# Fetching residual tiles one by one under two down products, and moving two tiles' LayerNorm statistics from VectorE to ScalarE

## The chip, the cores and the metric

One core of one Trainium2 chip. The metric is the device time of one execution in microseconds (us); lower is better. The kernel before takes 1430.34 us (median of 3 runs, 1430.0 to 1430.77). A verdict "faster" or "slower" needs 2%, 28 us; this study is about 2 us, so its conclusions rest on traces more than on times. In the lines of the profile PE is TensorE, PEld its weight loads, DVE VectorE, ACT ScalarE, POOL GpSimd and SPq the issuer of the DMA queue (SyncE); L428 is line 428 of the kernel, and brackets hold the idle time before an instruction and what ended it.

## The reference, cut to what matters

```python
x = A_x                                                  # 2048 x 1024, bf16
x = x + _A_ref(_layernorm(x, axis=-1), A_wqkv, A_wo)     # linear attention
x = x + _B_ref(_layernorm(x, axis=-1), B_w_gate, B_w_up, B_w_down)
x = x + _A_ref(_layernorm(x, axis=-1), A_wqkv, A_wo)
x = x + _B_ref(_layernorm(x, axis=-1), B_w_gate, B_w_up, B_w_down)
# _B_ref: g = x @ w_gate; u = x @ w_up; (g * u) @ w_down, inner width 3584
```

## The kernel before: the parts that matter

The tokens are 16 tiles of 128 rows. The multiplications of layer B are done with seven block products in place of eight, so PE has fewer columns to carry, at the price of additions and subtractions on VectorE. A layer B has two passes (`ps_` 0 and 1) over 8 tiles each: gate and up products, then a *down stage* of seven products in the order "1", "2", "6", "7", "4", "5", "3", four row tiles t each. That makes four down stages in a run. The residual tiles of a pass (`x_res`, 256 KB each) are overwritten as scratch space in the gate-up part of three of the four passes; they are stashed in DRAM and fetched back in the down stage.

All transfers that the kernel issues go through one queue (319.34 of the 320.74 MB in the profile; the rest is on two queues that it calls "instruction"), and SyncE issues them in the order in which the program has them (the burst below from 1107.59 us, the transposes behind it from 1112.33). The helper `P.add` records an instruction with what it reads and writes, and the waits follow from that.

```python
def tail(part):                     # end of the gate-up work, put under the first down product
    ...
    if part < 3:
        return
    for _ in range(2 if "R1" not in order else 1):
        ring_issue()                # weight fetches, 5 slots in a ring
    for t in range(8 if l2 and not jit else 0):
        i = 8 * ps_ + t
        dma(x_res[:, i, :], xscr[i * 128:(i + 1) * 128, :], r_x(i), KX[i], rd=R(V_X + i * 32, 32))

def evac(t, q=q):                   # after each row tile t of a product q
    ...
    if q == "1":
        P.add("act", ...copy bank to bank...)
        tt(hd, hd, hc, ALU.add, ...)             # two VectorE passes of 1.08 us
        tt(ha, hd, ha, ALU.subtract, ...)
    elif q in "24":
        stt(xs, pb, CD, a, ra_, rx, prd=[bank])  # residual tile += product
    elif q in "67":
        stt(rtmp[k], pb, CD, xs, rx, rr(k), prd=[bank])
        if q == "6":
            tt(hb, hb, ha, ALU.subtract, ...)
            tt(ha, hc, ha, ALU.subtract, ...)    # the operand of product "7"
    ...
    ticks(q, t)                     # in the first pass: lnp.flush_step() under "1" and "2"
    l2_ops(q, t)                    # operands of later products
```

`flush_step` finishes the LayerNorm of the last tiles in three steps: statistics (`start`; VectorE's BN_STATS, or two ScalarE passes with an accumulator, `ln_s1` and `ln_s2`: 1.06 and 1.15 us, each with 0.19 us for a separate instruction that reads the accumulator), normalize (`b2_one`, on VectorE, into one of a few buffers), and a transpose by the DMA engines (`step_t`) which reads that buffer. Tile 14 is normalized into the buffer that the transpose of tile 12 reads.

Of the kernel before, what the change touches and what calls it, by code (L numbers as in the profile page):

```python
# [180 lines left out]
def build_kernel(nc, A_x, A_wqkv, A_wo, B_w_gate, B_w_up, B_w_down, out):  # L181
# [97 lines left out]
    V_X = TOTAL + 64  # L279
# [46 lines left out]
    with ExitStack() as es:  # L326
# [82 lines left out]
        def R(o, n):  # L409
            return [(o, o + n)]  # L410

        def r_x(i, lo=0, hi=D):
            return [(O_X + (i * D + lo) * 2, O_X + (i * D + hi) * 2)]
# [13 lines left out]
        def dma(dst_ap, src_ap, wr, key, rd=()):  # L427
            P.add("sp", lambda e: e.dma_start(dst_ap, src_ap), rd=rd, wr=wr, dma_sem=key)  # L428
# [71 lines left out]
        class LN:  # L500
# [21 lines left out]

            def start(self, i, mid=None):
                assert i == self.n
                if self.to == "A0" and i in LN_ACT or self.to == "A" and i < 12:
                    j = ln_s1(self.order[i], *self.junk(i))
                    self.q_s.append((i, j))
                else:
                    j = ln_a(self.order[i], mid)
                self.n += 1  # L530
                self.q_b.append((i, j))
# [98 lines left out]

            def flush_step(self):
                self.step_t(1)
                if self.q_n:
                    self.b2_one()
                    self.b1_one()
                else:
                    self.b1_one()
                    self.b2_one()
                if self.n < NST and self.pending_ab() < 3:
                    self.start(self.n)  # L640

# [741 lines left out]
        def layer_B(lnp, nxt, first):  # L1383
# [207 lines left out]
            def gateup(ps_, ticks, l2):  # L1591
                jit = first and ps_ == 0
                NP = NU // 2
                pairs = [pair(ps_, p, l2) for p in range(NP)]

                def step(p, q, i):
                    L = pairs[p]["L"]
                    if q in L:
                        L[q]["st%d" % i]()

                order = ORDERS[not first, ps_].split()

                def sums(p, q):
                    if p < NP:
                        pairs[p]["sums"](q, "make" if first else "load")

                n0 = ps_ * NPASS

                pre = ("P1A", "P1B", "P5A", "P5B")
                tpl = tp_ops(ps_, l2)  # L1610
                todo = [(q, k) for q in dict.fromkeys(tk[0] for tk in order if tk[0] in l2) for k in range(4)]
                plain = set()

                def tp_next(q0=None):
                    for q, k in list(todo):
                        if (q == q0) if q0 else (k < 3 or q in plain):
                            assert k < 3 or q in plain
                            todo.remove((q, k))
                            tpl[q][k]()
                            if not q0:  # L1620
                                return

                def emit(p, tk, head=False):
                    late_ = tk[-1] == "'"
                    if late_:
                        p, tk = p - 1, tk[:-1]
                    if p < 0:
                        return
                    if p == 0 and not head and tk in pre:
                        if late_ and tk[:2] == "P5":  # L1630
                            pairs[0]["c22"]("AB".find(tk[-1]))
                        return
                    if p == 1 and tk[0] in l2 and tk[1] == "1":
                        tp_next(tk[0])
                    c, x = pairs[p], "AB".find(tk[-1])
                    if tk[0] == "P":
                        c["p" + tk[1]](x)
                    elif tk[0] == "D":
                        c["fin"](tk[1], x)()
                    elif tk[0] in "1245":  # L1640
                        step(p, tk[0], int(tk[1]))
                    elif tk[0] == "R":
                        if p or tk == "R1":
                            ring_issue()
                    elif tk == "W":
                        wd_dma()
                    elif tk[0] == "S" and not (early and p == 0):
                        sums(p + (tk[2] == "+"), tk[1])
                    elif tk[0] == "T":
                        i = int(tk[1])  # L1650
                        if jit:
                            store_s(n0 + 2 * p + i)
                            if p + 1 < NP:
                                prep_s(n0 + 2 * p + 2 + i)
                        ticks(2 * p + i)
                    if p == 0 and tk in ("P1B", "P5B", "D2B", "D4B") and tk[1] in l2:
                        plain.add(tk[1])
                    if p == 0 and not head:
                        tp_next()

                early = not first
                if early:
                    for q in "25"[ps_:]:
                        sums(1, q)
                for tk in pre:
                    emit(0, tk, True)
                if ps_ == 0:
                    lnp.b2_one()
                    lnp.start(13)
                for p in range(NP):  # L1670
                    for tk in order:
                        emit(p, tk)

                late = [tk for tk in order if tk[-1] == "'"]
                late = [tk for tk in late if tk[:2] == "D2"] + [tk for tk in late if tk[:2] != "D2"]
                nd2 = sum(tk[:2] == "D2" for tk in late)

                def tail(part):
                    n = -(-(len(late) - nd2) // 3)
                    lo, hi = (0, nd2) if part == 0 else (nd2 + n * (part - 1), min(nd2 + n * part, len(late)))  # L1680
                    for tk in late[lo:hi]:
                        emit(NP, tk)
                    if part < 3:
                        return
                    for _ in range(2 if "R1" not in order else 1):
                        ring_issue()
                    for t in range(8 if l2 and not jit else 0):
                        i = 8 * ps_ + t
                        dma(x_res[:, i, :], xscr[i * 128:(i + 1) * 128, :], r_x(i), KX[i], rd=R(V_X + i * 32, 32))
                return tail  # L1690

            def down(ps_, ticks, tail):
# [150 lines left out]
                for qi, q in enumerate(DPROD):  # L1843
# [17 lines left out]
                    def evac(t, q=q):  # L1861
                        pb, bank = psb((B_DX if q in "1674" else B_DV)[t]), (B_DX if q in "1674" else B_DV)[t]
                        ha, hb, hc, hd = [v[:, :, t * 128:(t + 1) * 128] for v in (hA, hB, hC, hD)]
                        ra, rb, rc, rd_ = [rh(x, t) for x in (O_HA, O_HB, O_HC, O_HD)]
                        if q == "1":
                            P.add("act", (lambda d, b: lambda e: e.copy(psb(d), psb(b)))(B_DV[t], bank), prd=[bank], pwr=[B_DV[t]])
                            tt(hd, hd, hc, ALU.add, rd_ + rc, rd_)
                            tt(ha, hd, ha, ALU.subtract, ra + rd_, ra)
                        elif q in "24":
                            sh = "24".index(q)  # L1870
                            xs, rx = xq(sh, 0, t)
                            a, ra_ = r4[t] if q in l2d else (xs, rx)
                            stt(xs, pb, CD, a, ra_, rx, prd=[bank])
                            final(sh, 0, t)
                        elif q in "67":
                            sh = "67".index(q)
                            xs, rx = xq(sh, 1, t)
                            k = t if sh else 4 + t
                            stt(rtmp[k], pb, CD, xs, rx, rr(k), prd=[bank])
                            if q == "6":  # L1880
                                tt(hb, hb, ha, ALU.subtract, ra + rb, rb)
                                tt(ha, hc, ha, ALU.subtract, ra + rc, ra)
                        else:
                            sh = "35".index(q)
                            xs, rx = xq(sh, 1, t)
                            k = t if sh else 4 + t
                            stt(xs, pb, CD, rtmp[k], rr(k), rx, prd=[bank])
                            final(sh, 1, t)
                        ticks(q, t)
                        l2_ops(q, t)  # L1890

                    if q in l2d:
# [178 lines left out]
```

## Time and profile before

| | kernel before |
|---|---|
| time | 1430.34 us |
| span of the profiled run | 1429.3 us |
| PE busy | 1421.5 us, 99% |
| PE idle between its first and last matmul | 3.8 us |
| of it in the last layer's first down stage | 1.66 + 0.50 us |
| a residual tile, issue to landing, median | 6.1 us |

The lines that carry this, and how they are read, are in the prediction.

### The profile page before, as it was taken

The page shows a single profiled execution, that of the slowest core. Times are in us where ns is not written, and L with a number is a line of the kernel's source. Part 1 is how long each engine was busy: PE and PEld are TensorE (multiplying, and loading weights), DVE is VectorE, ACT ScalarE, POOL GpSimd, SP SyncE. Part 2 cuts the span into 40 slices and gives each one's busy share as a digit, 9 for nine tenths or more (in the row PEclk, how much of TensorE's full clock was granted, in tenths as well). Part 3 has the DMA queues.
Part 4 walks back from the last instruction along what each step waited for, and adds up shares of the span by engine and source line. Part 5 has one row for each costly group of instructions (what it writes and reads, how often), then busy time and mean ns, then how long its engine had stood idle before and what let it go on. Part 6 is the DMA issues. An engine that isn't in the chain of part 4 may idle for free.

```text
span 1429.3 us, 21974 instructions
## 1 busy us (share of the span) xinstructions
PE 1421.5 (99%) x8209; PEld 790.0 (55%) x8209; DVE 1205.5 (84%) x2356; ACT 712.5 (50%) x1455; POOL 154.5 (11%) x193
## 2 busy tenths in 40 slices
PE   9999999999999999999999999999999999999999
PEld 4444444555546566664554444456666475666548
DVE  7897978999888799987689978888888787888888
ACT  5882355444410266655377714567775004777400
POOL 3203521000010000002010045300000100000000
PEclk9999999999999999999999999999999999999999
DMA  7868979997786776769784366767775976777653
GB/s 237 222 142 221 217 177 203 300 316 265 251 263 211 239 255 243 257 222 303 230 280 104 101 173 167 167 197 259 245 255 197 273 255 231 257 263 254 208 194 122
DMA packets 270699, 320.74 MB, mean 224 GB/s; under 512 B 164096, under 2 KB 211072, under 8 KB 270592
## 3 DMA queue, kind: packets, MB, share of 16 engines
q1 hardware_dynamic: 270592, 319.34, 73.1%
q8 instruction: 64, 1.05, 0.3%
q14 instruction: 43, 0.35, 0.1%
HBM read 236.45 MB, written 73.40 MB: 217 GB/s over the span
## 4 chain that ended last, share of the span: by engine, by line
PE 86%; DVE 7%; issue 2%; ACT 2%; POOL 1%; DMA 1%; SPq 0%; POOLq 0%; DVEq 0%
PE ps L1419 28%; PE ps L1502 17%; PE ps L1854 13%; PE ps L1235 8%; PE ps L974 8%; PE ps L1761 6%; PE ps L1337 4%; DVE arena L806 3%; DVE arena L455 2%; PE ps L947 1%; DMA arena<-arena 1%; DVE arena L809 1%; POOL arena L466 1%; PE ps L1261 1%; PE ps L1288 0%
## 5 line engine op out<-in xcount | busy, mean ns | idle before, releaser
L806 DVE TENSOR_TENSOR arena<-arena 128x512 f16<-128x512 f16 (+7 forms) x1027 | 507.2, 522 | 57.2 <-ACT arena L1506 32.7
L1419 PE MATMUL ps<-arena 128*128 128x512 f16 x1888 | 457.1, 379 | 0.5 <-DVE arena L809 0.4
L809 DVE SCALAR_TENSOR_TENSOR arena<-ps,arena 128x512 f16<-128x512 f32 (+3 forms) x558 | 358.4, 658 | 76.8 <-PE ps L1854 36.8
L1502 PE MATMUL ps<-arena 128*128 128x256 f16 x2184 | 287.5, 273 | 0.0
L1419 PEld LDWEIGHTS ps<-arena 128*128 128x128 f16 (+1 forms) x1888 | 182.6, 98 | 163.2 <-ACT ps L1448 3.8
L1502 PEld LDWEIGHTS ps<-arena 128*128 128x128 f16 (+1 forms) x2184 | 211.9, 98 | 90.6 <-ACT arena L1506 6.9
L1854 PE MATMUL ps<-arena 128*128 128x512 bf16 (+1 forms) x1064 | 232.6, 379 | 1.7 <-DVE arena L806 1.7
L1854 PEld LDWEIGHTS ps<-arena 128*128 128x128 f16 x1064 | 103.8, 98 | 125.9 <-DVE arena L806 2.2
L1424 ACT ACTIVATE arena<-ps 128x512 f32<-128x512 f32 x224 | 133.7, 597 | 76.8 <-PE ps L1419 62.9
L1506 ACT ACTIVATE arena<-ps 128x256 f32<-128x256 f32 x351 | 125.1, 384 | 26.4 <-PE ps L1502 21.5
L974 PE MATMUL ps<-arena 128*128 128x512 f16 (+1 forms) x616 | 134.7, 380 | 0.6 <-ACT arena L981 0.6
L1235 PE MATMUL ps<-arena 128*128 128x512 bf16 x512 | 116.1, 379 | 0.0
L1337 PE MATMUL ps<-arena 128*128 128x512 bf16 x512 | 110.8, 379 | 0.0
L1512 ACT COPY ps<-ps 128x256 f32<-128x256 f32 x182 | 66.4, 365 | 75.3 <-DVE arena L809 28.6
L974 PEld LDWEIGHTS ps<-arena 128*128 128x128 f16 x616 | 59.3, 98 | 74.9 <-ACT arena L981 5.8
L1761 PE MATMUL ps<-arena 128*128 128x256 f16 (+1 forms) x882 | 97.2, 273 | 0.5 <-DVE arena L809 0.5
L1448 ACT COPY ps<-ps 128x512 f32<-128x512 f32 x112 | 65.4, 584 | 62.2 <-PE ps L1419 51.9
L1076 POOL TENSOR_TENSOR arena<-arena 128x1024 f16<-128x1024 f32 x32 | 76.2, 2381 | 156.7 <-DVE arena L1074 141.2
L1761 PEld LDWEIGHTS ps<-arena 128*128 128x128 f16 x882 | 86.0, 98 | 11.9 <-DVE arena L809 1.0
L1515 DVE TENSOR_TENSOR ps<-ps,arena 128x256 f32<-128x256 f32 x182 | 76.7, 428 | 10.6 <-PE ps L1502 9.6
L1337 PEld LDWEIGHTS ps<-arena 128*128 128x128 f16 x512 | 50.0, 98 | 60.5
L1789 ACT COPY arena<-ps 128x256 f32<-128x256 f32 x8 | 3.0, 372 | 158.3 <-PE ps L1761 158.3
(72 smaller groups left out, 980.5 us busy)
## 6 DMA issues: line engine op xcount, KB each, us to landing
arena<-w_scratch SPq DMA_DIRECT2D x84, 896.0 KB, 4.5
arena<-t_scratch SPq DMA_DIRECT2D x32, 896.0 KB, 6.0
arena<-in_B_w_down_dram SPq DMA_DIRECT2D x24, 896.0 KB, 5.2
arena<-sp_scratch SPq DMA_DIRECT2D x26, 768.0 KB, 4.2
w_scratch<-arena SPq DMA_DIRECT2D x28, 512.0 KB, 6.2
arena<-w_scratch SPq DMA_DIRECT2D x28, 384.0 KB, 5.1
x_scratch<-arena SPq DMA_DIRECT2D x40, 256.0 KB, 5.0
arena<-x_scratch SPq DMA_DIRECT2D x40, 256.0 KB, 6.1
```

Of the source, the lines that this page charges most:

```text
L806: P.add("dve", lambda e: e.tensor_tensor(out=out, in0=a, in1=b, op=op), rd=rd, wr=wr, prd=prd)
L809: P.add("dve", lambda e: e.scalar_tensor_tensor(out=out, in0=a, scalar=sc, in1=b, op0=ALU.mult, op1=op1), rd=rd, wr=wr, prd=prd)
L974: P.add("pe", lambda e: [e.matmul(psb(bank), a[0][:, k, :], b[0][:, k, :], start=(q in (1, 5) and k == 0), stop=(k == 3), skip_group_check ...
L1235: return [e.matmul(psb(bank), xrt[t][:, jj * 128:(jj + 1) * 128], pk[:, h, t, :], start=(t == tok[0]), stop=(t == tok[NST - 1])) for t in ts]
L1337: return [e.matmul(psb(bank), xnT[:, g, i * 128:(i + 1) * 128], wp[:, g, dh * 512:(dh + 1) * 512], start=(dh == 0 and g == 0), stop=(g == ...
L1419: P.add("pe", lambda e: [e.matmul(psb(bank), w[:, k, :], x[:, k, :], start=(start and k == 0), stop=(k == 3), skip_group_check=True) for k ...
L1424: P.add("act", lambda e: e.activation(t, psb(bank), AF.Copy, scale=SG), prd=[bank], wr=r)
L1502: P.add("pe", lambda e: [e.matmul(psb(bank)[:, 256 * half:256 * half + 256], w[:, k, :], xx[:, k, :], start=(start and k == 0), stop=(k == ...
L1506: P.add("act", lambda e: e.activation(d, src, AF.Copy, scale=sc), prd=[xk], wr=rd_)
L1515: P.add("dve", lambda e: e.tensor_tensor(out=half(c, 1), in0=U, in1=c5, op=ALU.add), prd=[xk], rd=rc5, pwr=[dst[c]])
L1761: P.add("pe", lambda e: [e.matmul(psb(bank)[:, 256 * half:256 * half + 256], a[:, k, 128 * r:128 * r + 128], b[:, k, :], start=(start and ...
L1854: P.add("pe", lambda e: [e.matmul(psb(bank), hv[:, 7 * hf + k, t * 128:(t + 1) * 128], w[:, k, :], start=(q in "15" and hf == 0 and k == 0 ...
```

## The change

Intent: the burst of eight fetches stands in the queue ahead of the LayerNorm transposes and of later weights, so it is spread, one fetch for each row tile of products "1" and "2"; and the last two tiles' statistics leave VectorE (busy for 14.21 of the 22 us from 1105, and waiting for 6.31 more) for ScalarE (busy for 2.28 of them).

```diff
@@ LN.start
-                if self.to == "A0" and i in LN_ACT or self.to == "A" and i < 12:
+                if self.to == "A0" and i in LN_ACT or self.to == "A" and i < 12 or self.to == "B" and i >= 14:
                     j = ln_s1(self.order[i], *self.junk(i))
@@ LN.flush_step
                 self.step_t(1)
-                if self.q_n:
+                n = len(self.q_n)
+                if n:
                     self.b2_one()
+                if self.q_b and (not self.q_s or self.q_s[0][0] > self.q_b[0][0]):
                     self.b1_one()
-                else:
-                    self.b1_one()
+                if not n:
                     self.b2_one()
+                self.s2()
@@ tail
-                    for t in range(8 if l2 and not jit else 0):
-                        i = 8 * ps_ + t
-                        dma(x_res[:, i, :], xscr[i * 128:(i + 1) * 128, :], r_x(i), KX[i], rd=R(V_X + i * 32, 32))
@@ evac
                         ticks(q, t)
+                        if q in "12" and (ps_ or not first):
+                            i = i0 + 4 * "12".index(q) + t
+                            dma(x_res[:, i, :], xscr[i * 128:(i + 1) * 128, :], r_x(i), KX[i], rd=R(V_X + i * 32, 32))
                         l2_ops(q, t)
```

## The prediction

> **What bounds the kernel now.** I read the page's engine table first, then the waits of PE, then the waits of the one stretch that holds PE's longest idle time, and there the timeline engine by engine. From the page (engine, busy us, share of the span):
>
> ```profile
> span 1429.3 us, 21974 instructions
> PE 1421.5 (99%) x8209; PEld 790.0 (55%) x8209; DVE 1205.5 (84%) x2356; ACT 712.5 (50%) x1455; POOL 154.5 (11%) x193
> ```
>
> PE is idle for 1429.3 - 1421.5 = 7.8 us in all. A busy PE need not be a fast one, so I checked its pace: the timeline has 56 matmuls of 512 columns that take 12.26 us (the PE line at 1140.57 below). The last one's record is 0.38 us long, so the 55 steps before it take (12.26 - 0.38) / 55 = 216 ns each. Going through the start times of all 512-column matmuls gives a median of 216 ns and hardly any outlier. So PE runs at its pace everywhere, and the change removes no matmul. Of the 7.8 us, 1.4 us lie before the first matmul and 2.7 us after the last (it ends at 1426.6). What is left, 3.8 us, is all that any change of waits can win. The waits of PE over the whole run (waiter, what it waited for, us in total, times, longest):
>
> ```profile
> PE ps L1854 <- DVE arena L806: 1.7, 1, 1.7
> PE ps L435 <- POOL arena L431: 1.4, 1, 1.4
> PE ps L974 <- ACT arena L981: 0.6, 3, 0.2
> PE ps L1761 <- DVE arena L809: 0.5, 1, 0.5
> PE ps L1419 <- DVE arena L809: 0.4, 1, 0.4
> ```
>
> L1854 is a plain down product and L1761 a down product split once more: two of the waits, 1.7 and 0.5 us, belong to the code that the change touches. Both fall in the first down stage of the last layer, at 1138.9 and 1156.7 us. The waits of that stretch (1105 to 1160) name where they start:
>
> ```profile
> DVE arena L496 <- DMA arena<-arena: 6.3, 1, 6.3
> PEld ps L1854 <- DMA arena<-t_scratch: 0.2, 1, 0.2
> ```
>
> The timeline shows the sequence (start, duration, engine, line; SPq is the DMA queue's issuer):
>
> ```profile
> 1107.21 0.34 SPq L428 DMA_DIRECT2D arena<-t_scratch  x1
> 1107.59 4.39 SPq L428 DMA_DIRECT2D arena<-x_scratch  x8
> 1112.33 10.51 SPq L579 DMA_TRANSPOSE arena<-arena  x3
> 1121.04 0.55 DVE L496 TENSOR_SCALAR arena<-arena 128x1024 f16<-128x1024 bf16 x1 [6.31 <-DMA arena<-arena]
> 1122.89 1.06 SPq L428 DMA_DIRECT2D arena<-t_scratch  x2
> 1128.30 0.68 DVE L809 SCALAR_TENSOR_TENSOR arena<-ps,arena 128x512 bf16<-128x512 f32 x1
> 1138.30 2.21 DVE L806 TENSOR_TENSOR arena<-arena 128x1792 f16<-128x1792 f16 x2
> 1140.57 12.26 PE L1854 MATMUL ps<-arena 128*128 128x512 f16 x56 [1.66 <-DVE arena L806]
> ```
>
> Eight residual tiles (256 KB each, 2 MB) are issued in one go. The transpose of a LayerNorm tile that was ready goes out 4.7 us later, behind them; the normalize of tile 14 (L496) needs the buffer which that transpose reads, so DVE stands for 6.31 us. [...] all its later work slides: the evacuation of product "2" starts at 1128.30, and the two subtractions that make the operand of product "7" end at 1138.30 + 2.21 = 1140.5, where PE has been waiting since 1138.9.
>
> The first layer's first down stage is the control that the kernel itself contains: the same products, the same LayerNorm steps, but no fetch (its tiles were never overwritten). Same engines, same columns:
>
> ```profile
> 404.42 9.41 SPq L579 DMA_TRANSPOSE arena<-arena  x3
> 412.02 0.55 DVE L496 TENSOR_SCALAR arena<-arena 128x1024 f16<-128x1024 bf16 x1 [0.46 <-POOL arena L466]
> 419.27 0.68 DVE L809 SCALAR_TENSOR_TENSOR arena<-ps,arena 128x512 bf16<-128x512 f32 x1
> 429.28 2.21 DVE L806 TENSOR_TENSOR arena<-arena 128x1792 f16<-128x1792 f16 x2
> ```
>
> There the transposes go out at once, L496 does not wait for a DMA, and PE has no wait. PE's groups of product "1" are 701.67 us apart in the two layers (third row tile at 406.86 and 1108.53), so 419.27 corresponds to 1120.94: the last layer's DVE is 1128.30 - 1120.94 = 7.4 us later than the control. In the control the operand of product "7" is ready at 431.4 and product "7" starts at 437.1: 5.7 us of slack. 7.4 - 5.7 = 1.7 us, which is the wait on PE. So the wait is explained to 0.1 us or so.
>
> [...] an issue is 0.3 to 0.5 us, a residual tile takes a median of 6.1 us to land, and the two weight fetches at 1122.89 stood behind a transpose that waited for DVE.
>
> **The change part by part.** I compared the instruction order of both kernels on each engine.
>
> (a) The burst of eight fetches goes, in the three down stages that had it. One fetch follows each row tile of products "1" and "2". In the last layer's first down stage the queue becomes: weights, transpose 12, tile 0, transpose 13, tiles 1 and 2, two weights, transpose 14, tile 3, and so on. Transpose 12 then goes out at about 1107.6, as in the control at 404.42. The control's DVE found its buffer free 7.6 us later (412.02); here DVE needs it at about 1115.2 (worked out below), 7.6 us later too. So the 6.31 us go.
>
> (b) Statistics of tiles 14 and 15, in both layers: DVE loses two BN_STATS (1.42 us the pair) and one aggregate (0.21) for each tile, 2 x 1.63 = 3.3 us a layer. ACT gets for each tile a Copy pass and a Square pass with accumulators, which cost 1.06 + 0.19 and 1.15 + 0.19 us where the kernel has them already (median of 17 each): 2 x 2.6 = 5.2 us a layer. ACT has little else there but four copies of 0.57 us, one each 3 us. POOL gets three small ops for two. The last copy of product "1" moves back by perhaps 1 to 2 us to about 1116; its bank is written by PE from 1123.6. So nothing of (b) reaches PE.
>
> DVE's new timeline, last layer: normalize 13 at 1110.5 as now, then four subtractions of row tiles 1 and 2 (4 x 1.05) to 1115.2, normalize 14 to 1115.7, two subtractions to 1117.8, normalize 15. Its statistics: ACT sums tile 14 at 1106.9 to 1108.2, POOL negates (0.95) to 1109.3, ACT squares to 1110.9 and sums 15 to 1112.2; POOL finishes 14 (0.95 + 1.39) at about 1113.4 and negates 15 to 1114.4; ACT squares to 1115.9, POOL ends at about 1118.4. Normalize 15 thus waits some 0.7 us and ends at 1119.0, and product "2" is evacuated from there instead of 1128.3. From then on PE sets the pace: product "6", row 0, ends at about 1129.7, the operand of "7" is ready by 1132.7, and "7" starts at 1138.75: 6 us of slack.
>
> What PE wins: a wait costs the idle time plus the overlap that the pipeline loses, 0.380 - 0.216 = 0.164 us. First wait 1.664 + 0.164 = 1.83. The second (1156.7, product "4") comes while DVE still works off its backlog without a break; with 6 us of slack it goes as well: 0.498 + 0.164 = 0.66. Sum 2.49 us. In the other three down stages PE has no wait to lose. 1430.34 - 2.49 = 1427.85 us.
>
> **The rivals.** *A late residual tile becomes the new wait.* Tile 3 now stands behind two weight fetches (1.8 MB, about 8 us at the page's mean of 224 GB/s) and is needed when row 3 of "2" ends, near 1126.7; issued near 1117, it lands near 1123 to 1125. In the first layer's second stage it also stands behind three 512 KB fetches and may be some 3 us late for 668.5. DVE would wait, but the operand of "7" has about 6 us of slack in each case (there ready at 674.3, used at 680.4). For it: the DMA share is 1.03 of full in 1107 to 1131. Effect on the time: nothing, or up to 1 us. *Only the first wait goes*, because the dense DVE work of product "7" makes the second by itself: 1428.5. Against it: the control has the same work and no such wait. *The burst was harmless elsewhere and something else takes the place of the transpose* (accumulating passes late, normalize 15 held for several us): DVE may be late by up to 6 us before PE sees it, so 1428 again. *The drop in DVE load gives much more*: not possible, since PE has only 3.8 us of waits. A slowdown of 2% would need 28 us of new waits on PE; only the queue held for long at one blocked fetch could do that, and each fetch here waits for scratch areas whose last reader has already run.
>
> **Range and chances.** The three timed runs of before lie within 0.8 us, half of it above the median. Lower end: all 2.5 us and 0.6 us of luck, 1427.2. Upper end: the first wait goes, the second stays or a new one of 0.5 to 1 us comes: 1429.3. The gain is 0.17%, so "within 2%" is all but certain.
>
> **What would show it.** Right: in the last layer's first down stage the transposes follow the weight fetch at once, L496 waits for no DMA there for more than 1 us, the evacuation of "2" starts near 1119, and PE's waits on DVE at L1854 and L1761 are gone, with PE's idle time near 5.6 us. Wrong: a wait of DVE on x_scratch longer than 6 us, a PE wait on L1854 or on a weight fetch in any of the four down stages, or L496 waiting for POOL for several us.

Its sum is: 1.83 + 0.66 = 2.49 us, so 1427.85 us. That PE can do no better than 216 ns a step at 512 columns was not shown; the forecast rests only on the change leaving that pace alone (median 216 ns in both kernels). That the transpose of tile 12 is late behind the burst was measured: 8.6 us from issue to landing behind the 2 MB, 5.7 us in the first layer's stage, 6.7 us in the changed kernel. VectorE started nothing in the 6.31 us in which it waited, and evacuated product "2" 7.4 us later than in the first layer.

## The result, and the profile after

The changed kernel takes 1428.59 us (median of 4 runs, 1428.16 to 1429.18), the kernel before 1430.55 us beside it: 1.96 us less. The ratio is 0.9987, 95% interval 0.997 to 1.0004. Ratios here are the mean time of one kernel's fast runs over that of the other's of the same rounds, so not quite the ratio of the medians.

The page of the changed kernel:

```profile
span 1426.4 us, 21923 instructions
PE 1417.6 (99%) x8150; PEld 791.0 (55%) x8209; DVE 1200.9 (84%) x2344; ACT 722.0 (51%) x1471; POOL 153.8 (11%) x197
```

PE has 59 matmul records fewer (8150 against 8209) and as many weight loads. These records are missing, not the work (eleven of the twelve traces here lack 59); each leaves a false gap of 0.053 us, 3.1 us in all, so PE's true idle time is 8.8 - 3.1 = 5.7 us. VectorE is busy 4.6 us less and ScalarE 9.5 us more; added up record by record (records on one engine overlap, by 0.08 us at 1121.5 in the kernel before) it is 6.2 and 10.5 us, near the prediction's 6.6 and 10.4.

The waits of PE over the whole run now show nothing from a down stage:

```profile
PE ps L435 <- POOL arena L431: 1.4, 1, 1.4
PE ps L943 <- DMA arena<-in_A_wqkv_dram: 0.7, 2, 0.5
PE ps L976 <- ACT arena L983: 0.6, 3, 0.2
```

Lines shift by up to two between the kernels: L809 became L811, L1854 became L1853. The timeline of the same stage, DMA queue and VectorE:

```profile
1106.57 0.34 SPq L428 DMA_DIRECT2D arena<-t_scratch  x1
1106.96 1.24 SPq L579 DMA_TRANSPOSE arena<-arena  x1
1108.24 0.71 SPq L428 DMA_DIRECT2D arena<-x_scratch  x1
1113.68 0.91 SPq L428 DMA_DIRECT2D arena<-t_scratch  x2
...
1114.62 0.54 DVE L496 TENSOR_SCALAR arena<-arena 128x1024 f16<-128x1024 bf16 x1
1117.66 0.68 DVE L811 SCALAR_TENSOR_TENSOR arena<-ps,arena 128x512 bf16<-128x512 f32 x1
1129.85 2.21 DVE L808 TENSOR_TENSOR arena<-arena 128x1792 f16<-128x1792 f16 x2
```

The transpose follows the weights at once, normalize 14 waits for nothing, product "2" is evacuated 10.6 us earlier than before (0.6 us of it the scatter below), and the operand of product "7" is ready at 1132.1, some 6 us before PE takes it up.

**Where the time went.** All 8209 weight loads of PE have a record in every trace, in the same order, so the start times of two traces, each counted from the start of its span, can be subtracted one by one. After minus before:

| stretch of PE's stream | change, us |
|---|---|
| start to the last layer's first down stage | -0.6, most of it near 242 us |
| first wait, product "7" | -1.84 |
| second wait, product "4" | -0.67 |
| near 1319 us | +0.26 |
| end | -2.88 |

The -0.6 us lie before anything that the change touches: ScalarE's instructions first differ at 405 us. In the eleven other traces that stretch is between 0.6 us shorter and 1.1 us longer than in the first trace of the kernel before, without pattern: that is the scatter from run to run. The +0.26 us were not expected.

### The profile page after: what moved, and what is told of

Its sections match the earlier page's. It is cut to its first block, busy times and chain, and to the rows that moved or that the text cites. A ratio compares the mean times of both kernels' runs of the same rounds, so it can differ in the third digit from the quotient of the medians.

```text
span 1426.4 us, 21923 instructions
## 1 busy us (share of the span) xinstructions
PE 1417.6 (99%) x8150; PEld 791.0 (55%) x8209; DVE 1200.9 (84%) x2344; ACT 722.0 (51%) x1471; POOL 153.8 (11%) x197
## 4 chain that ended last, share of the span: by engine, by line
PE 92%; DVE 4%; ACT 2%; issue 1%; DMA 1%; POOL 0%; SPq 0%; DVEq 0%
PE ps L1421 29%; PE ps L1504 17%; PE ps L1853 16%; PE ps L1339 8%; PE ps L1237 8%; PE ps L976 8%; PE ps L1760 5%; DVE arena L808 1%; PE ps L949 1%; DVE arena L811 1%; DVE arena L455 1%; ACT arena L668 1%; DMA arena<-in_A_wqkv_dram 1%; PE ps L1263 1%; PE ps L1290 0%
## 5 line engine op out<-in xcount | busy, mean ns | idle before, releaser
L811 DVE SCALAR_TENSOR_TENSOR arena<-ps,arena 128x512 f16<-128x512 f32 (+3 forms) x558 | 358.6, 658 | 86.9 <-PE ps L1853 45.0
L1853 PE MATMUL ps<-arena 128*128 128x512 bf16 (+1 forms) x1048 | 230.6, 379 | 0.8
L1853 PEld LDWEIGHTS ps<-arena 128*128 128x128 f16 x1064 | 104.1, 98 | 123.8
```

What stands on the lines that cost most here:

```text
L811: P.add("dve", lambda e: e.scalar_tensor_tensor(out=out, in0=a, scalar=sc, in1=b, op0=ALU.mult, op1=op1), rd=rd, wr=wr, prd=prd)
L1853: P.add("pe", lambda e: [e.matmul(psb(bank), hv[:, 7 * hf + k, t * 128:(t + 1) * 128], w[:, k, :], start=(q in "15" and hf == 0 and k == 0 ...
```

## The experiments

Each lists its edit, the expectation before the run, and what came. "Stage" is the change of PE's start times over the last layer's first down stage, against the first trace of the kernel before; unrounded, it is -2.505 to -2.508 us in all eight traces that have -2.51 (the changed kernel's first trace is the eighth).

| run | DVE waits for a transpose, us | stage, us | median, and of before beside it, us | ratio |
|---|---|---|---|---|
| e1_fetch_only | 0 | -2.51 | 1428.82, 1431.03 | 0.9986 |
| e2_stats_only | 4.8 | -2.51 | 1428.99, 1431.03 | 0.9988 |
| e3_burst_behind | 0 | -2.51 | 1428.77, 1431.03 | 0.9986 |
| e4_burst_twice | 10.6 | +4.29 | 1435.40, 1431.03 | 1.0031 |
| e5_half_burst | 1.5 | -2.51 | 1428.95, 1430.93 | 0.9988 |
| e6_dve_plus5 | 0 | -2.51 | 1428.95, 1430.93 | 0.9986 |
| e7_dve_plus10 | 0 | +0.88 | 1431.90, 1430.93 | 1.0008 |
| after_again | 0 | -2.51 | 1429.26, 1430.93 | 0.9989 |
| before_again | 5.5 | -0.86 | 1430.75, 1430.29 | 1.0003 |
| e8_act_pad | 0 | -2.51 | 1428.40, 1430.29 | 0.9988 |

All outputs are right.

### Each half alone

e1: the burst goes and the one-by-one fetches come, as in the change; `start` and `flush_step` stay as before.

```diff
-                    for t in range(8 if l2 and not jit else 0): ...dma(x_res...)      # in tail
+                        if q in "12" and (ps_ or not first): ...dma(x_res...)         # in evac
```

> Fetches one by one as in the change, statistics of tiles 14 and 15 left on DVE. Theory (the burst holds the LayerNorm transpose, DVE stands 6.3 us, its lag of 7.4 us exceeds the 5.7 us of slack): the stage becomes like the first layer's, DVE's wait for the transpose falls below 1 us, the evacuation of product 2 starts near 1121, both PE waits (1.66 and 0.50 us) go, time 2.5 us below the kernel before (ratio 0.9983). Rival 'the relief of DVE by the statistics did it': the 6.3 us may go, but the PE waits stay at least in part, gain under 1 us.

Measured: both PE waits are gone, stage -2.51 us. VectorE's only waits at L496 are two of 0.46 us for POOL. It evacuates product "2" at 1122.32, 1.3 us later than expected and without effect.

e2: the two LN edits of the change, with the burst left in `tail`.

```diff
+ ... or self.to == "B" and i >= 14:      # LN.start, and flush_step as in the change
```

> Statistics of 14 and 15 on ACT as in the change, the burst of eight fetches kept where it was. Theory: DVE still waits for the transpose, until about 1121 (some 4 us now, since four subtractions stand before normalize 14 in place of two), but after that it has 1.6 us of statistics, 2.1 us of subtractions and 0.5 us of a POOL wait less; evacuation of product 2 near 1124.1, lag 3.2 us against 5.7 us of slack: both PE waits go as well, time 2.5 us below before. So each half alone gives the whole gain, and the two do not add. Rival 'only the order of transfers matters': DVE's wait stays, PE keeps a wait of 1 to 2 us at the down product, gain under 1 us.

Measured: stage -2.51 us although VectorE still stands behind the burst. Its timeline:

```profile
1121.22 0.55 DVE L496 TENSOR_SCALAR arena<-arena 128x1024 f16<-128x1024 bf16 x1 [4.78 <-DMA arena<-arena]
1124.27 0.68 DVE L811 SCALAR_TENSOR_TENSOR arena<-ps,arena 128x512 bf16<-128x512 f32 x1
```

What follows: the halves do not add. Counted from the same start of the stage, product "2" is evacuated 5.9 us earlier than in the kernel before with e1 and 5.1 us earlier with e2. Each is more than the 1.7 us by which VectorE was over its slack, so either is enough, and the other then buys slack that PE does not need. The rival for e1 ("the relief of VectorE did it") and that for e2 ("only the order of transfers matters") both fall.

### The burst kept, but put behind the transposes

```diff
-                    for t in range(8 if l2 and not jit else 0): ...          # in tail
+                        if q == "1" and t == 1 and (ps_ or not first):       # in evac
+                            for i in range(i0, i0 + 8):
+                                dma(x_res[:, i, :], ...)
```

> All eight fetches still in one burst, but issued behind the transposes of tiles 12 and 13 (after row tile 1 of product 1); statistics on DVE. Theory (place in the queue, not the burst): DVE waits under 1 us for the transpose, no PE wait, 2.5 us below before. Rival 'bandwidth' (the DMA share is 1.03 in the stretch, so 2 MB at once delay whatever is needed then): DVE waits 4 us or more on a transpose, a residual tile or PE on a weight fetch, and PE keeps a wait of 1 us or more.

Measured: stage -2.51 us. The DMA queue:

```profile
1108.24 4.75 SPq L579 DMA_TRANSPOSE arena<-arena  x2
1113.03 5.39 SPq L428 DMA_DIRECT2D arena<-x_scratch  x8
```

The same 2 MB in one burst do no harm 5 us later. The place in the queue matters, not the burst, and not the bandwidth; fetching "one by one" is one of several ways to get the transposes out first.

### More and less of the burst

e4: sixteen transfers ahead of the transposes, in the last layer's first down stage alone.

```diff
-                    for t in range(8 if l2 and not jit else 0):
-                        i = 8 * ps_ + t
+                    for t in range((16 if is_last and not ps_ else 8) if l2 and not jit else 0):
+                        i = 8 * ps_ + t % 8
```

> Kernel before, with the eight tiles of the last layer's first down stage fetched twice (16 transfers ahead of the transposes; the second set waits for the first to land). Theory: the transpose lands 8 to 12 us later still, DVE's wait grows from 6.3 to 14 to 18 us and PE's first wait by as much, from 1.7 to 10 to 14 us: time 8 to 12 us above before. Rival 'PE's wait has another cause than the place of the transpose in the queue': time unchanged within 2 us.

Measured: direction right, size wrong, and PE's wait of another kind. VectorE's wait grew by 4.3 us, to 10.6 (the issue of sixteen took 10.9 us against 4.4; by an estimate from the 6.1 us that a residual tile takes from issue to landing in the kernel before, the first eight were landing meanwhile). PE's waits of the stage:

```profile
PE ps L1854 <- DMA arena<-t_scratch: 3.8, 1, 3.8
PE ps L1761 <- DVE arena L809: 0.5, 1, 0.5
PE ps L1854 <- DVE arena L806: 0.3, 1, 0.3
```

The weights of product "6" (issued from 1127.75, before: 1122.89) stand in the queue behind the transpose of tile 14, which waits for VectorE, which waits for the transpose of tile 12: lateness on VectorE comes back as late weights. In the kernel before the same path held up a weight load by 0.2 us (the PEld wait in the prediction), and PE not at all. The waits are 4.6 us, with 3 x 0.164 us of lost overlap 5.1; the stage lost 4.29 + 2.49 = 6.8 us against no wait at all. The rest is PE's clock. The windows view (stretch; the last three columns are granted clock, DMA share, GB/s):

```profile
1128.00:1132.70 4.70, 0.89 (x5) 0.19 (x2) 4.17 (x6) 0.00 (x0) 2.33 (x2) 1.00 1.01 301
1132.70:1136.20 3.50, 3.47 (x11) 1.33 (x12) 3.50 (x5) 0.00 (x0) 0.00 (x0) 0.62 1.08 352
```

From 0.9 us after the wait of 3.84 us, eight matmuls start 0.427 us apart in place of 0.216, which is 1.7 us. PE had been idle for 3.84 us, and the granted clock was 0.5 for 3.413 us. After the waits of 1.7 us, in the kernel before and in e7, the pace did not drop. At what idle time it begins to drop is not shown.

e5: four tiles ahead of the transposes, the others one by one under product "2".

```diff
-                    for t in range(8 if l2 and not jit else 0):
+                    for t in range(4 if l2 and not jit else 0):
+                        if q == "2" and (ps_ or not first):                  # in evac
+                            i = i0 + 4 + t
+                            dma(x_res[:, i, :], ...)
```

> Statistics on DVE; four residual tiles in one burst ahead of the transposes, the other four one by one under product 2. From the DVE waits measured so far (0 tiles ahead: none beyond POOL's 0.5 us, 8: 6.3, 16: 10.6) half the burst should cost DVE 2 to 4 us. Theory: evacuation of product 2 near 1124 to 1126, just within the slack, so no PE wait, stage 2.5 us shorter than before. Rival 'PE's wait grows in step with the burst': about half of the wait stays, 1 to 1.5 us.

Measured: VectorE waits 1.5 us (less than expected), PE not at all. For PE the dose is a threshold, not a slope: 0, 4, 8 and 16 tiles ahead of the transpose cost VectorE 0, 1.5, 6.3 (5.5 in the second trace) and 10.6 us, and PE saw only the last two.

### VectorE made late without any transfer

The changed kernel with useless BN_STATS at the end of product "1", in that one stage: 7 in e6, 14 in e7.

```diff
                         ticks(q, t)
+                        if is_last and not ps_ and q == "1" and t == 3:
+                            for _ in range(7):                               # 14 in e7
+                                P.add("dve", lambda e: e.bn_stats(st[7][:, 0:6], x_res[:, 12, 0:512]), ...)
```

> The changed kernel with 7 useless BN_STATS (0.71 us each, 5.0 us) on DVE at the end of product 1 in the last layer's first down stage. Theory: PE sees DVE only when it is more than about 8 us later than in the changed kernel (its evacuation of product 2 starts at 1117.7; PE would wait from about 1125.9 on), so no PE wait, time unchanged within 0.5 us. Rival 'PE follows DVE closely there': 2 to 5 us longer.

Measured: 5.1 us of useless work on an engine that is busy 84% of the span, and no PE wait; stage -2.51 us and a time (1428.95) between those of the changed kernel.

> The same with 14 BN_STATS, 9.9 us: evacuation of product 2 at about 1127.6, where it was in the kernel before (1128.3 less the 0.6 us by which the whole profile is earlier), but with transposes and weights early. Theory (DVE's lag alone makes the waits): PE's waits come back as they were, 1.7 and 0.5 us within 0.3 us, stage 2.3 to 2.5 us longer than in the changed kernel, time as before. Rival 'late weights made a part of it': the waits come back smaller, under 1 us in all.

Measured: with 10.2 us, the first wait is back at 1.73 us (before: 1.66), so lateness of VectorE alone makes it. The second did not come back as 0.5 us; another one took its place. PE's timeline:

```profile
1141.33 1.69 PE L1853 MATMUL ps<-arena 128*128 128x512 f16 x7 [1.73 <-DVE arena L808]
1144.33 10.75 PE L1853 MATMUL ps<-arena 128*128 128x512 f16 x49 [1.31 <-DMA arena<-t_scratch]
```

Seven matmuls into product "7", PE waits for the second half of its weights. They were issued at 1136.37, after the residual fetches, output stores and stashes that alternate with product "2"'s evacuations, and PE got them 8 us later. In the kernel before the same weights were issued at 1135.07 and landed 5.2 us later, 1.8 us before PE needed them. In the changed kernel the fetches of tiles 4 to 6 stand ahead of them too, but there they are issued at 1127.01 and land 6.7 us before PE needs them. The rival expected smaller waits and falls as well: together they were larger, 3.0 us against 2.2, and the stage became 3.4 us longer than in the changed kernel, where 2.3 to 2.5 us had been expected.

### How far one trace speaks for all runs

> The changed kernel once more, unedited, with five rounds. The stage's two PE waits add up to 2.50 us in the trace; the first timing gave 1.96 us between medians. Expected: ratio 0.9983 to 0.9988 and again neither wait; the 0.26 us that the first profile lost near 1318 (a ScalarE copy starts 0.35 us after the record of its wait in place of 0.06) appears again if it comes from the place of the instruction in ScalarE's stream, and not if it is chance.

Measured: no PE wait in the stage, and 1.67 us between the medians (1.96 the first time). The loss near 1319 us came again, 0.25 us. So one part of the shortfall is real. The other:

> The kernel before once more, unedited, to see how far one trace of it speaks for all its runs. If the two PE waits (1.66 and 0.50 us) are there again within 0.1 us, the 2.5 us stand and the smaller timed difference (1.5 to 2.2 us) is scatter from elsewhere; if they differ by 0.5 us or more, the wait itself scatters with the DMA and the single trace overstated it. Ratio 1.000 within 0.0005.

Measured: the first wait was 0.8 us in place of 1.7. PE's waits, and VectorE's, in this second trace of the unedited kernel before:

```profile
PE ps L1854 <- DVE arena L806: 0.8, 1, 0.8
PE ps L1761 <- DVE arena L809: 0.5, 1, 0.5
```

```profile
DVE arena L496 <- DMA arena<-arena: 5.5, 1, 5.5
```

The transpose landed 0.8 us earlier, and PE's wait shrank by as much, as it must when VectorE is over its slack. The wait that the change removes is itself a random quantity; the trace that the prediction was made from shows it large. That this run's median is 0.46 us above that of its twin shows the size of timing noise with five to nine runs.

### The 0.26 us near 1319

ScalarE has a bank-to-bank copy there that PE soon needs. The timeline of the changed kernel's second trace, and then that of e1 at the same place of the algorithm (in brackets: idle time before it, and what ended it):

```profile
1318.12 0.36 ACT L1514 COPY ps<-ps 128x256 f32<-128x256 f32 x1 [1.12 <-PE ps L1504]
```

```profile
1317.79 0.36 ACT L1512 COPY ps<-ps 128x256 f32<-128x256 f32 x1 [0.84 <-DVE arena L809]
```

The first had been idle 0.28 us longer. The raw records show the wait's own event 0.336 us ahead of the copy in the first and 0.057 us in the second. All five traces with the statistics on ScalarE had it (0.336 to 0.350 us, always at record 1599 of ScalarE, counted from 0), the six without them (both of the kernel before, e1, e3, e4, e5) did not. The edit, on the changed kernel:

```diff
+                        if is_last and not ps_ and q == "1" and t == 3:
+                            for _ in range(5):
+                                P.add("act", lambda e: e.copy(vf(O_B6, 1), mhalf), ...)
```

> The changed kernel with five one-column copies on ScalarE at the end of product 1 of the last layer's first down stage, where ScalarE is idle. The wait of 0.26 us near 1318 came in every profile with the statistics on ScalarE (three of the changed kernel's form and two with more DVE work) and in none without. If it hangs on where an instruction stands in ScalarE's stream, it goes away or moves with five more instructions ahead of it, and PE then is 2.5 us earlier than in the kernel before at the end of the last layer; if it belongs to the accumulating passes themselves, it stays at the same copy. Time not above the changed kernel's, difference under 0.3 us either way.

Measured: with five useless instructions more on ScalarE the copy starts 0.057 us after the event again, and from the start of the stage to the end of the run PE gains 2.51 us on the kernel before (2.26 in the second trace of the changed kernel). So the delay hangs on the place of an instruction in ScalarE's stream, not on what the passes do. The traces of the kernel before support this: they have the same delay elsewhere. At 573 us, record 575 of ScalarE, the same kind of copy starts 0.336 or 0.350 us after its wait's event in the six traces without the statistics on ScalarE; in the six with them there is no such delay at that copy. There it costs PE 0.03 us. So the delay is not new with the change: it comes at another place, one where PE feels it. Not every place that was looked at has it: records 319, 1087 and 1343 of the changed kernel waited too and started 0.02 us after the update that they waited for. What is at the place stays open. The median of e8, 1428.40, is the lowest, but its ratio (0.9988) is that of the others; at this size the times can't rank e1, e3, e8 and the changed kernel.

## Why the prediction was right, and what it mis-sized

- *The bound.* Right. PE had 3.8 us of waits in all, and the stage gave 2.5 us in every version without a wait there, never more; the changed kernel's idle time is 5.7 us (5.6 expected).
- *The chain: burst, transpose, VectorE, operand of "7", PE.* Shown link by link: the queue (e3), the dose (e4, e5), VectorE alone (e7), and the two traces of the kernel before, in which transpose and PE wait move by the same 0.8 us.
- *The slack.* The control in the first layer gave 5.7 us, and the changed kernel was said to stand lateness of up to 6; e6 used up 5.1 us without effect, e7 overran with 10.2. The 6 us were too few: in e7 product "2" was evacuated 10.1 us late and PE waited 1.7, so some 8.3 us were absorbed (an estimate from these two). The prediction counted from the time at which the operand of "7" is ready, and left out that VectorE idles before that, 2.1 us in the changed kernel. It erred on the safe side.
- *"So nothing of (b) reaches PE."* Half right. It gave no gain beside the fetches, as said. But it would have been enough alone (e2), which the prediction did not see, and it costs 0.26 us at a far place, by shifting ScalarE's instructions.
- *The size.* Expected 2.49 us, measured 1.96 and 1.67. The mis-sized term is the first wait, "1.664 + 0.164 = 1.83". A second trace has 0.803 + 0.164 = 0.97, mean 1.40. An estimate from both traces, 1.40 + 0.66 - 0.26 = 1.80 us, agrees with the two timings (mean 1.8). The range held (1428.59 within 1427.2 to 1429.3) because its upper end allowed for a wait that stays or a new one; that the shortfall came from a first wait that scatters, and from ScalarE, was not foreseen.
- *Rival "late residual tile".* Seen where it was looked for, in the first layer's second stage, and absorbed as said (up to some 3 us had been expected). VectorE's wait there, after:

```profile
DVE arena L811 <- DMA arena<-x_scratch: 1.3, 1, 1.3
```

- *Smaller misses.* Normalize 15 was to wait 0.7 us for POOL and did not: POOL negated the sum of tile 14 in 0.41 us, where 0.95 had been taken from another of its instructions.

## What to carry to other kernels

In a kernel that is bound by one engine at 99%, sum that engine's waits before you judge a change: the sum, with the overlap lost at each, is the most that any reordering can give, and here the idle time was 0.26% of the whole. What an engine off the path is late by counts only beyond its slack, so two cures for the same lateness do not add; when transfers share one queue, put the small one that an engine stands on ahead of the large ones that nobody needs yet (VectorE's wait here: 6.3 us behind eight tiles, none ahead of them). When the gain is a wait on a transfer, look at two traces before you size it.
